# Attention between two expert stages: one reduction on VectorE issued a step earlier, a fourth buffer for the split exponentials, and a small scaling moved to GpSimd

## The chip, the cores and the metric

One core of a Trainium2 chip. The metric is the device time of one execution in microseconds (us), here the median of three. The engines are TensorE (PE in the profile; PEld its weight loads), VectorE (DVE), ScalarE (ACT), GpSimd (POOL) and SyncE (SP), which issues most of the DMAs.

## The reference

Cut to what matters: eight heads of attention over 576 positions for a batch of two, with a bias that comes from a small network over relative positions, and then two pairs of dense layers over the 1152 tokens.

```python
scores = np.matmul(q, k.transpose(0, 1, 3, 2)) / np.sqrt(D)    # B=2, H=8, S=576, D=64
scores = scores + bias.transpose(2, 0, 1)[None]                # bias: a 32-wide net over positions
scores = scores - np.max(scores, axis=-1, keepdims=True)
attn = np.exp(scores)
attn = attn / (np.sum(attn, axis=-1, keepdims=True) + 1e-09)
x = np.matmul(attn, v)                                         # -> [1152, 512]
h = x @ w_in; x = (P(h) / (Q(h) + 1e-6)) @ w_out               # 512 -> 2048 -> 512, rational function
h = x @ w_in2; out = np.maximum(0.01 * h, h) @ w_out2          # 512 -> 2048 -> 512
```

## The kernel before

The program has three stretches. Up to about 60 us it builds the bias tables. From there to about 212 us it runs attention. The rest, two thirds of the time, is the two dense stages, which TensorE fills. Single-precision products are made of three half-precision or rounded products (a high and a low part of each operand).

**Units, tiles and steps.** Attention works on eight units; a unit is a pair of heads in one batch. A unit has nine score tiles: four blocks of 128 rows for each of the two heads (tiles 0 to 7), and a ninth with the last 64 rows of both. The loop goes over all 72 tiles in order, one tile a step, so a unit takes nine steps. Here "step m of a pass" is the step in which the tile number m of the pass's unit is reduced; pass u belongs to unit u.

At each step the program issues, in this order: `qk` of the next tile (six matmuls, line 751, into one of two PSUM slots), `ttr` of this tile (VectorE, line 763: adds the bias, finds the row minimum), `hi` of the tile before (the exponentials rounded to 16 bits into the tile `hl`, ScalarE line 801 or VectorE line 803), `lo` of the tile before that (the remainder of that rounding, line 816, mostly GpSimd, in part VectorE), then the background work due at the step, and `exps` of this tile (ScalarE, line 779). Each engine runs what was issued to it strictly in that order.

**The split exponentials.** Two tiles share one `hl` buffer. When both of its `lo` are done SyncE issues one DMA transpose (line 822) from `hl` into `et`, which the product with v reads later. A `hi` that opens a new `hl` buffer waits until the transpose out of the buffer's former contents has landed. There are `NHL` = 3 such buffers of 4,608 bytes in each partition.

**Background work.** `PLAN` lists it: an entry (step, name) runs for unit i at step 9i + step. The entries that the change and the prediction touch:

- `v_sum` (line 686), now at -4: five matmuls (line 691) that form the squares of v's entries, and a VectorE reduction of the diagonal (line 694), written to `vsc`. It writes and reads a spare corner of `pr`, the PSUM tile of unit i-2. At the same step, and issued ahead of it, stand `rbc` of unit i-2 (twelve short matmuls in the profile, lines 870 and 872) and `prep_q` (ScalarE, line 670).
- `v_scale` (line 698) at -3: one matmul pair (line 701) sums `vsc` over the partitions, ScalarE makes a scale of it (lines 702 and 703). `prep_v8` (line 707) and `prep_vd` (line 711) use the scale at steps 1 and 2 of the unit's own pass.
- `prep_k` at -2 (ScalarE line 682, GpSimd line 683), `prep_ql` at -3 and -1 (VectorE line 675).
- `rmul` (line 885) and `xlo` (line 894), both VectorE, at the step where `rsum` stands.
- `rsum` at 9, that is step 0 of the next pass: a VectorE `tensor_scalar` (line 849) over the nine row sums of the unit, 128 x 9 numbers. `rrec` (line 853), one step later on VectorE, takes the reciprocal, and `rbx` (line 859) one step after that turns it for the rows' normalisation.

For the first two units `v_sum` and `v_scale` stand elsewhere (in the bias stretch), and the last two units take their `rsum` from a second list, `TAIL`. So `PLAN` issues six `v_sum` (units 2 to 7), in passes 1 to 6, and six `rsum` (units 0 to 5), also in passes 1 to 6.

Of the kernel before, what the change touches and what calls it, by code (L numbers as in the profile page):

```python
# [15 lines left out]
ALU = mybir.AluOpType  # L16
# [189 lines left out]
def arrange(tasks, ends, free, shift, slack):  # L206
# [22 lines left out]
    while todo:  # L229
# [36 lines left out]
GROUPS_0 = [[(0, 0), (0, 1)], [(1, 0), (1, 1)], [(2, 0), (2, 1)], [(3, 0), (3, 1)], [(8, 2)]]  # L266
AV_ORDER = (0, 1, 2)
RBX_ACT = True
NHL = 3
LAG_HI, LAG_LO = 1, 2  # L270
PLAN = [(-24, 'load_part', 0), (-22, 'load_part', 1), (-20, 'load_part', 2), (-18, 'load_part', 3), (14, 'rbc'), (17, 'av', 2, 0, 1), (22, 'xhi'), (-2, 'prep_k'), (18, 'rmul'),
        (16, 'av', 1, 0, 1), (1, 'prep_v8'), (-3, 'v_scale'), (17, 'rev'), (11, 'rbx'), (-4, 'v_sum'),
        (12, 'av', 0, 0, 1), (10, 'rrec'), (-1, 'prep_ql', 1), (2, 'prep_vd'), (27, 'xlo'),
        (-4, 'prep_q', 0), (9, 'rsum'), (-2, 'prep_q', 1), (-3, 'prep_ql', 0)]
TAIL = [(2, 'rbx', 0), (3, 'rbc', 0), (2, 'w_load', -2, 0), (1, 'av', 0, 0, 0, 1), (0, 'rsum', 0),
# [73 lines left out]
def attn_bias_moe_kernel(  # L349
# [13 lines left out]
    V, A, G, PE, SP = nc.vector, nc.scalar, nc.gpsimd, nc.tensor, nc.sync  # L363
# [286 lines left out]
    st_q, st_v, kts, ets, vds, vscs = {}, {}, {}, {}, {}, {}  # L650
# [64 lines left out]
    with att, ExitStack() as st:  # L715
# [4 lines left out]
        s_ps, s_pt, s_hl, sums, xx = {}, {}, {}, {}, {}  # L720
# [20 lines left out]
        def kind(i):  # L741
            return (i > 0) + (i == len(units) - 1)
# [49 lines left out]
        def hi(i, j):  # L792
            if group_of[kind(i), j][0] == 0:
                s_hl[i] = hlp.tile([128, most, 2 * S], F16, tag="hl", name="hl", bufs=NHL)
            s_hl[i, j] = s_hl[i]
# [50 lines left out]

        def rsum(i):
            r9 = opn.tile([128, 9], F32, tag="r9", name="r9", bufs=2)
            V.tensor_scalar(r9, sums.pop(i), 1e-9, vscs[i][:, 1:2], ALU.add, ALU.mult)
            r9s[i] = r9  # L850

        def rrec(i):
# [38 lines left out]
        def xlo(i, c=None):  # L891
# [6 lines left out]
        nu = len(units)  # L898
        ops = {
            f.__name__: f  # L900
            for f in (load, load_part, prep_v8, prep_vd, prep_q, prep_ql, prep_k)
            + (av, rsum, rrec, rbx, rbc, rev, rmul, xhi, xlo)
        }

# [131 lines left out]

        hlp = st.enter_context(tc.tile_pool(name="hlp", bufs=NHL))
        etp = [st.enter_context(tc.tile_pool(name=f"etp{x}", bufs=1)) for x in range(2)]
# [363 lines left out]
```

## Time and profile before

| | |
|---|---|
| median of 3 runs | 640.57 us (638.73 to 642.4) |
| the profiled execution | 638.54 us, its span 636.7 us |
| TensorE, VectorE, ScalarE, GpSimd busy over the span | 90%, 86%, 69%, 43% |
| mean granted TensorE clock | 0.973 |

How to read it: the busy shares are means over stretches with different limits, so the part that the change touches is read by itself, in windows of some 17 to 19 us. A row of the timeline is start, duration, engine, line, what it writes and reads, and in brackets how long the engine stood idle before it and what it waited for. A profiled execution is 1.84 us longer than its span.

### The profile page before, as it was taken

What the parts mean: (1) busy time and instruction counts of PE and PEld (TensorE: products, weight loads), DVE (VectorE), ACT (ScalarE), POOL (GpSimd) and SP (SyncE); (2) the same over time, 40 slices, a digit from 0 to 9 for tenths busy, and PEclk for the clock granted to TensorE, in tenths of its full rate; (3) what the DMA queues carried; (4) which work ended last, traced back from release to release, by engine and by line L of the source; (5) the groups of instructions that cost most, each with busy time, mean ns of one, the idle gap of its engine ahead of it and who ended that gap; (6) DMA issues with size and microseconds to landing.
All of it is one profiled execution on the core that took longest, in us unless ns stands there. A gap on an engine that the chain in (4) does not pass through costs nothing.

```text
span 636.7 us, 10678 instructions
## 1 busy us (share of the span) xinstructions
PE 572.0 (90%) x4042; PEld 431.6 (68%) x4042; DVE 545.2 (86%) x818; ACT 438.5 (69%) x705; POOL 270.9 (43%) x194
## 2 busy tenths in 40 slices
PE   4889698888897866799999999999899999999997
PEld 1335577777786756699999999987555555555543
DVE  7997877888887679889999999889897888988684
ACT  8998888888897558898777778648767443444320
POOL 2000866677666124667656766540332112112110
PEclk9999799898999977999999999999999999999999
DMA  6889999999789420132131211031313132131003
GB/s 221 221 219 252 191 174 195 190 190 207 135 162 203 138 99 34 66 113 86 67 133 44 90 67 67 33 133 68 132 71 129 67 117 81 67 132 67 1 0 148
DMA packets 103796, 76.58 MB, mean 120 GB/s; under 512 B 86585, under 2 KB 89145, under 8 KB 103746
## 3 DMA queue, kind: packets, MB, share of 16 engines
q1 hardware_dynamic: 103026, 71.91, 43.7%
q10 hardware_dynamic: 720, 4.00, 1.9%
q8 instruction: 31, 0.51, 0.4%
q14 instruction: 19, 0.16, 0.1%
HBM read 41.69 MB, written 2.36 MB: 69 GB/s over the span
## 4 chain that ended last, share of the span: by engine, by line
PE 50%; DVE 21%; ACT 16%; DMA 6%; issue 5%; SPq 0%; POOL 0%; DVEq 0%; ACTq 0%
PE ph L528 20%; PE pz L1150 14%; PE py L1088 10%; DMA et<-hl 3%; PE ps L751 3%; ACT ex L779 3%; DMA bias<-bb 3%; DVE s L605 2%; DVE pt L763 2%; DVE raw L443 2%; ACT mk L984 2%; DVE raw L441 2%; ACT hl L801 2%; ACT ah L564 1%; DVE mk L986 1%
## 5 line engine op out<-in xcount | busy, mean ns | idle before, releaser
L816 POOL TENSOR_TENSOR hl<-ex,hl 128x512 f16<-128x512 f32 (+2 forms) x94 | 91.0, 986 | 85.4 <-DVE hl L803 54.5
L528 PE MATMUL ph<-bias,bias 128*128 128x384 f32 x576 | 108.6, 346 | 11.6 <-DVE s L602 9.4
L528 PEld LDWEIGHTS ph<-bias,bias 128*128 128x128 f32 x576 | 104.5, 196 | 13.8 <-issue 10.3
L528 PE MATMUL ph<-x,w 128*128 128x384 f16 x576 | 102.0, 326 | 2.1 <-ACT w L489 1.4
L1150 PE MATMUL pz<-w,g 128*128 128x512 f16 (+1 forms) x438 | 101.4, 376 | 1.5 <-DVE bias L1169 1.5
L632 POOL TENSOR_TENSOR g<-s,g 128x1152 f16<-128x1152 f32 x16 | 38.5, 2406 | 144.4 <-ACT g L628 144.4
L751 PE MATMUL ps<-kt,qz 128*128 128x288 f32 x432 | 79.8, 326 | 20.7 <-DVE mn L763 13.9
L751 PEld LDWEIGHTS ps<-kt,qz 128*128 128x128 f32 x432 | 63.6, 200 | 33.8 <-DVE mn L763 18.0
L528 PEld LDWEIGHTS <-w 128*128 128x128 f16 x576 | 55.3, 98 | 45.4 <-issue 4.9
L1088 PE MATMUL py<-gh,wo 128*128 128x384 f32 x288 | 79.9, 340 | 1.7 <-ACT gh L618 1.3
L1150 PEld LDWEIGHTS <-g 128*128 128x128 f16 x438 | 42.7, 98 | 47.2 <-issue 2.0
L779 ACT ACTIVATE ex<-pt,mn 128x576 f32<-128x576 f32 x72 | 55.2, 767 | 9.7 <-DVE mn L763 9.3
L1169 DVE SCALAR_TENSOR_TENSOR bias<-pz,inv,bias 128x512 f32<-128x512 f32 x56 | 41.8, 747 | 22.1 <-PE pz L1150 19.0
L1088 PEld LDWEIGHTS py<-gh,wo 128*128 128x128 f32 x288 | 52.6, 188 | 5.2 <-DVE bias L1100 3.3
L763 DVE CUSTOM_DVE_ANT_0 pt<-ps,bias 128x576 f32<-128x576 f32 x64 | 47.5, 744 | 6.5 <-PE ps L751 2.3
L1088 PE MATMUL py<-gl,wo 128*128 128x384 f32 x156 | 52.2, 335 | 0.0
L599 POOL TENSOR_TENSOR qq<-qq,r 128x1152 f32<-128x1152 f32 (+1 forms) x17 | 41.2, 2429 | 19.0 <-ACT qq L593 14.7
L986 DVE TENSOR_SCALAR mk<-te,off 128x576 f32<-128x576 f32 x108 | 47.1, 507 | 0.0
L439 DVE TENSOR_SCALAR raw<-biasr 128x1024 int32<-128x1024 int32 (+1 forms) x36 | 39.7, 1104 | 6.2 <-DMA biasr<-in_moe_w_in 5.5
L623 POOL TENSOR_TENSOR gl<-s,gh 128x1152 fp32r<-128x1152 f32 (+1 forms) x17 | 41.1, 2427 | 9.0 <-ACT gh L618 8.8
L443 DVE SCALAR_TENSOR_TENSOR raw<-biasr,raw 128x1024 int32<-128x1024 int32 (+1 forms) x36 | 42.2, 1173 | 0.9
L441 DVE SCALAR_TENSOR_TENSOR raw<-biasr,raw 128x1024 int32<-128x1024 int32 (+1 forms) x36 | 40.5, 1126 | 0.7
(131 smaller groups left out, 1095.9 us busy)
## 6 DMA issues: line engine op xcount, KB each, us to landing
biasr<-in_moe_w_in SPq DMA_DIRECT2D x32, 512.0 KB, 4.1
biasr<-in_moe_w_out SPq DMA_DIRECT2D x32, 512.0 KB, 3.2
bias<-bb SPq DMA_DIRECT2D x32, 288.0 KB, 4.7
qkv<-in_qkv ACTq DMA_DIRECT2D x4, 896.0 KB, 7.3
qkv<-in_qkv SPq DMA_DIRECT2D x16, 224.0 KB, 3.1
out<-bias SPq DMA_DIRECT2D x8, 256.0 KB, 2.0
biasr<-bb SPq DMA_DIRECT2D x8, 144.0 KB, 4.6
et<-hl SPq DMA_TRANSPOSE x40, 4.9
```

What stands on the lines that cost most here:

```text
L441: V.scalar_tensor_tensor(bits, hi32, -0x40000000, bits, ALU.bitwise_and, ALU.bitwise_or)
L443: V.scalar_tensor_tensor(bits, lo32, 29, bits, ALU.logical_shift_right, ALU.bitwise_or)
L528: PE.matmul(ps[:, c, 0:CH], w[:, sl], x[kk][:, c * CH:(c + 1) * CH], start=(kk == 0 and n == 0), stop=(kk == KD - 1 and n == 2),)
L599: G.tensor_tensor(part(qq[f], c), part(qq[f], c), part(r0[f], c), ALU.mult)
L751: PE.matmul(ps[:, c, 0:288], lt[:, a], kts[i][:, b, 288 * c:288 * c + 288], start=(n == 0), stop=(n == 2),)
L763: V.tensor_tensor_reduce(out=c2(pt), in0=s_ps.pop((i, j))[:, :, 0:288], in1=c2(bsrc), op0=ALU.add, op1=ALU.min, scale=1.0, scalar=3.0e38, ...
L779: A.activation(et, pt, AF.Exp, bias=mn, scale=-1.0, accum_out=sums[i][:, col:col + 1],)
L816: engines[j in at].tensor_tensor(hl[:, xs, dst], e9[:, xs, src], hl[:, xs, src], ALU.subtract)
L986: V.tensor_scalar(mk, src, off[:, col], 0.0, ALU.add, ALU.max)
L1088: PE.matmul(ps[:, 0:CH], w[:, sl], gts[f][x][:, cs], start=(f == f0 and m == 0), stop=(f == f0 + nf - 1 and m == 2),)
L1150: PE.matmul(ps[:, part], gts[f][x][:, sl], w[:, part], start=(f == f0 and m == 0), stop=(f == f0 + nf - 1 and m == 2),)
L1169: V.scalar_tensor_tensor(dst, ps[:, part], back, dst, ALU.mult, ALU.add)
```

## The change

Three edits, each in one place:

- `NHL` goes from 3 to 4: a fourth `hl` buffer; the tiles that are laid out behind it in the partition move up by 4,608 bytes.
- `v_sum` goes from step -4 to -5. At that step only `xhi` (ScalarE, line 889) of unit i-3 stands ahead of it; `rbc` and `prep_q` of step -4 now come after it. `v_scale` stays at -3.
- `rsum` of units 0 to 5 is issued to GpSimd; units 6 and 7 stay on VectorE. `rrec` stays on VectorE and now has to wait for GpSimd.

```diff
-NHL = 3
+NHL = 4
 PLAN = [...
-        (16, 'av', 1, 0, 1), (1, 'prep_v8'), (-3, 'v_scale'), (17, 'rev'), (11, 'rbx'), (-4, 'v_sum'),
+        (16, 'av', 1, 0, 1), (1, 'prep_v8'), (-3, 'v_scale'), (17, 'rev'), (11, 'rbx'), (-5, 'v_sum'),
...
         def rsum(i):
             r9 = opn.tile([128, 9], F32, tag="r9", name="r9", bufs=2)
-            V.tensor_scalar(r9, sums.pop(i), 1e-9, vscs[i][:, 1:2], ALU.add, ALU.mult)
+            (G if i < nu - 2 else V).tensor_scalar(r9, sums.pop(i), 1e-9, vscs[i][:, 1:2], ALU.add, ALU.mult)
             r9s[i] = r9
```

## Rows read from the trace of the kernel before

**Rows 1.** Busy by pass 3 to 6: window; length, PE PEld DVE ACT POOL; clock; DMA

```profile
111.05:130.03 18.98, 16.56 (x166) 13.88 (x160) 15.90 (x35) 15.87 (x35) 13.04 (x14) 0.91 1.05 189
130.03:147.43 17.40, 15.03 (x161) 12.80 (x159) 15.34 (x35) 15.47 (x34) 13.23 (x14) 1.00 0.98 196
147.43:166.48 19.05, 16.69 (x166) 14.00 (x160) 15.14 (x35) 15.73 (x34) 12.73 (x14) 0.91 0.99 179
166.48:183.94 17.46, 15.08 (x165) 12.87 (x160) 15.30 (x35) 15.66 (x35) 13.21 (x14) 1.00 0.80 151
```

**Rows 2.** Waits from 75 to 200 us: waiter <- releaser, total us, times, longest

```profile
PE ps L751 <- DVE mn L763: 11.7, 14, 2.0
DVE vd L694 <- PE pr L691: 10.7, 6, 1.8
...
ACT vsc L702 <- PE pr L701: 3.1, 3, 1.1
...
ACT hl L801 <- DMA et<-hl: 2.7, 3, 2.1
DVE hl L803 <- DMA et<-hl: 2.0, 3, 1.2
```

**Rows 3.** Timeline of VectorE: `rsum` of pass 2, then of pass 3, and what follows

```profile
94.39 0.23 DVE L849 TENSOR_SCALAR r<-sums,vsc 128x9 f32<-128x9 f32 x1
...
95.21 0.77 DVE L803 CAST hl<-ex 128x576 f16<-128x576 f32 x1
...
96.02 0.69 DVE L763 CUSTOM_DVE_ANT_0 pt<-ps,bias 128x576 f32<-128x576 f32 x1
...
113.22 1.12 DVE L849 TENSOR_SCALAR r<-sums,vsc 128x9 f32<-128x9 f32 x1
114.26 0.74 DVE L763 CUSTOM_DVE_ANT_0 pt<-ps,bias 128x576 f32<-128x576 f32 x1
...
114.94 0.45 DVE L803 CAST hl<-ex 128x576 f16<-128x576 f32 x1
...
115.43 0.69 DVE L763 CUSTOM_DVE_ANT_0 pt<-ps,bias 128x576 f32<-128x576 f32 x1
```

**Rows 4.** Timeline of GpSimd at the same two places

```profile
94.50 4.86 POOL L816 TENSOR_TENSOR hl<-ex,hl 128x512 f16<-128x512 f32 x5 [0.19 <-POOL hl L816]
...
112.67 1.91 POOL L816 TENSOR_TENSOR hl<-ex,hl 128x512 f16<-128x512 f32 x2 [0.20 <-POOL hl L816]
```

**Rows 5.** The chain that ended last, in order of time: one piece, in pass 4

```profile
132.25 1.04 DVE r L849
```

**Rows 6.** Timeline of TensorE after `rsum`: pass 3, then pass 6

```profile
115.06 1.45 PE L751 MATMUL ps<-kt,qz 128*128 128x288 f32 x6 [1.98 <-DVE mn L763]
...
170.50 1.05 PE L751 MATMUL ps<-kt,qz 128*128 128x288 f32 x6 [1.98 <-DVE mn L763]
```

**Rows 7.** Timeline of TensorE in pass 1, steps 5 to 7

```profile
86.66 0.46 PE L691 MATMUL pr<-qkv 128*128 128x128 bf16 x5
86.93 1.04 PE L751 MATMUL ps<-kt,qz 128*128 128x288 f32 x6
87.81 0.28 PE L701 MATMUL pr<-vsc,ones 128*128 128x1 f32 x2
88.28 0.90 PE L751 MATMUL ps<-kt,qz 128*128 128x288 f32 x5 [0.20 <-DVE mn L763]
```

**Rows 8.** Timeline of ScalarE, pass 2: its longest wait for a buffer

```profile
103.67 0.69 ACT L801 ACTIVATE hl<-ex 128x576 f16<-128x576 f32 x1 [2.09 <-DMA et<-hl]
```

**Rows 9.** GpSimd's groups by form over the span: busy us, mean ns | idle before

```profile
L683 POOL TENSOR_TENSOR kt<-qkv,kt 128x576 fp32r<-128x576 f32 x8 | 12.2, 1522 | 12.1 <-ACT kt L682 12.1
L816 POOL TENSOR_TENSOR hl<-ex,hl 128x64 f16<-128x64 f32 x23 | 9.2, 399 | 0.0
...
L962 POOL MEMSET tiny<- 128x1 f32 x1 | 0.1, 108 | 0.0
```

**Rows 10.** GpSimd's first TENSOR_TENSOR of the execution, in the timeline

```profile
8.73 2.06 POOL L683 TENSOR_TENSOR kt<-qkv,kt 128x576 fp32r<-128x576 f32 x1 [5.46 <-ACT kt L682]
```

## The prediction

> **What bounds the kernel now.** The dense stages are TensorE's and hold nothing that the edits touch; they only start earlier or later. So I first cut attention into passes. There [rows 1] no engine is full: in a pass of 17.40 us ScalarE is busy for 15.47, VectorE 15.34, TensorE 15.03, GpSimd 13.23. The pass is a ring of four engines that hand each other tiles, and what counts is which wait ends last at each place. Two things are to be seen. Passes 3 and 5 last 18.98 and 19.05 us, 4 and 6 only 17.40 and 17.46, at nearly the same work: in the long ones the granted TensorE clock is 0.91 on average and TensorE is busy 1.5 to 1.7 us longer. And the list of waits [rows 2] is led by TensorE waiting for the row minimum (11.7 us) and by VectorE waiting for the five matmuls of `v_sum` (10.7 us). The first is a loss. The second looks like one, and the chain has to say whether it is: it holds `rsum`, as a piece of 1.04 us [rows 5], while around `v_sum` it runs through ScalarE or TensorE, not through VectorE.
>
> **rsum.** Nine numbers per partition should be cheap: in pass 2 the instruction takes 0.23 us. In pass 3 it takes 1.12 us [rows 3], and so in four of the six passes that are changed (3 to 6). In pass 2 it started just ahead of GpSimd's `lo`; in pass 3 `lo` had been running since 112.67, 0.55 us before it [rows 4]. So it stood behind GpSimd's instruction. The next tile's reduction came 1.04 us late (113.22 to 114.26), TensorE stood idle for 1.98 us at just this place [rows 6], and ScalarE's next exponential waited too.
>
> Removing it frees 1.04 us of VectorE, but not all stays free. After the next reduction VectorE casts (`hi` of tile 0), and in pass 2, where `rsum` slipped through, that cast took 0.77 us rather than 0.45 [rows 3]: the wait for GpSimd is handed on. From the start of `rsum` to the reduction after the cast it is 2.21 us in pass 3 and 1.63 in pass 2. So one bound of the gain is 2.21 - 1.63 = 0.58 us a pass, the other 1.04. TensorE and ScalarE wait for the earlier reduction, which gains the whole 1.04, VectorE's own line for the later one; I take 0.8, in four passes 3.2 us. In passes 1 and 2 at most the 0.23 goes: together 0.3. Sum 3.5, bounds 2.3 and 4.6.
>
> [...]
>
> On GpSimd the trace shows no tensor_scalar. The nearest rows are a fill of one column, 0.108 us, and a two-operand instruction of 64 columns, 0.399 us [rows 9]. Nine columns are nearer the former; I take 0.2, six times 1.2 us of GpSimd. What hides it: GpSimd is free for 4 us of a pass [rows 1]. Queued behind it are `lo` of tile 8 and its transpose, read much later by the product with v; without that cover it would cost the 1.2 us, 2.4 by the upper row. `rrec` on VectorE now waits for GpSimd. `rsum` can run when `lo` of tile 7 ends, 0.20 us before 112.67 [rows 4]; VectorE comes to `rrec` between the cast (114.94) and the reduction at 115.43 [rows 3], or 1.04 earlier if all the gain arrives. That is over 1 us of slack, so I cost the new wait at nothing; an instruction of more than 1.5 us would use it up.
>
> **TensorE's clock.** In pass 3, behind the 1.98 us of idleness, six matmuls took 1.45 us; in pass 6, behind the same 1.98, they took 1.05 [rows 6]. The drop to the lower of the two levels follows such a wait in two passes of four. In a long pass it costs 16.56 - 15.03 = 1.53 or 16.69 - 15.03 = 1.66 us of TensorE. If the wait shrinks to about 1 us, the drop should become rarer. I take half of the two drops, 1.5 us; bounds 0 and 3.1.
>
> **v_sum.** VectorE's 1.8 us a pass is the largest number here, and I count almost nothing of it. TensorE's order in steps 5 to 7 is `rbc`, `v_sum`, scores of tile 7, `v_scale`, scores of tile 8 [rows 7]. Moved, it is `v_sum`, scores of tile 6, `rbc`, scores of tile 7, `v_scale`: the same matmuls in sum, so the scores of tile 7 end at the same time, and so does `v_scale`, for which ScalarE waits in three passes (3.1 us in all [rows 2]). Those three are passes in which TensorE came late. VectorE reduces tile 6 some 1.5 us earlier, and then waits for the scores of tile 7 instead: what is late next is TensorE. What remains is the 0.20 us that the scores of tile 8 wait for the reduction of tile 6 [rows 7]; six times that is 1.2. Against it, the reduction of v now stands ahead of tile 5's and holds that back a little, covered by ScalarE's queue; uncovered, the 0.27 us of `v_sum` on TensorE (86.66 to 86.93) would be lost six times, 1.6. I take a gain of 0.4, bounds -1.6 and 1.2. No DMA moves with it, and neither SyncE's nor GpSimd's queue is passed.
>
> **The fourth buffer.** Waits for a buffer are 2.7 us on ScalarE and 2.0 on VectorE [rows 2], most of it one wait of 2.09 us in pass 2 [rows 8]. It lies on ScalarE, which is then busy without a gap, and VectorE's wait for `v_sum` at that place, which would have been next, goes too: of that wait I count 1.4. The rest lies where TensorE is late: 0.2. Sum 1.6, bounds 0.4 and 3.5. The tiles that move by 4,608 bytes change which earlier tiles lie under them; no row prices that, and no edge of attention waits for such a tile visibly, so I cost it at nothing.
>
> **Sum.** 3.5 + 1.5 + 0.4 + 1.6 = 7.0 us. The profiled execution took 638.54, so it would be 631.5; the median of the runs lies 2.03 higher: 633.5 us. The bounds together are a gain of 1.1 (2.3 + 0 - 1.6 + 0.4) and 12.4 (4.6 + 3.1 + 1.2 + 3.5). About 0.5% (3.2 us) is what a measurement of this kernel can tell from no change, that is 637.4 to 643.8.
>
> **Rivals.**
>
> The gain is taken up by the ring. ScalarE is busy for 15.5 to 15.9 us of a pass [rows 1]; if its queue, and not the reduction, sets passes 4 and 6, only the small bound of `rsum` (2.3) and of the buffer (0.4) come through, less part of GpSimd's 1.2: 1 to 3 us, 637.5 to 639.5. For it: in passes 4 and 6 ScalarE is the busiest engine. Against it: ScalarE itself waits for the reduction behind `rsum`.
>
> The clock falls more often, and the kernel becomes slower. Shorter waits elsewhere shift where TensorE is idle; the place is the wait after `rsum` or one newly made before the scores of tile 6. The price of a drop is 1.5 to 1.7 us. Without the clock's term the gain is 5.5, so four drops more, one in each of the passes that have none, take it away, and six more, the last of them at the edge to the dense stage, make it slower by 0.5%: 641 to 645. Against it: pass 6 has none at the longest wait [rows 6].
>
> GpSimd's first tensor_scalar costs a start. Its first two-operand instruction took 2.06 us [rows 10] where the mean of that line is 1.52 [rows 9]: 0.5 us once, 634. [...]
>
> All terms come through in full: 12 us, 628 to 629.
>
> **Chances.** The forecast (629.5 to 637.4) 0.54; all in full 0.08; taken up by the ring 0.23, an eighth of it still under 637.4; GpSimd's start 0.05; clock and slower 0.10, of which 0.07 over 643.8. So faster by over 0.5%: 0.65, within: 0.28, slower: 0.07. The likeliest is 633.5. A range of 628.5 to 641 leaves out about 0.05 below and 0.10 above.
>
> **What the profile after would show.** `rsum` on GpSimd at 0.1 to 0.4 us, and no wait of `rrec` for it. TensorE's wait for the row minimum after it near 1 us instead of 1.98, the cast longer. No wait of `v_sum`'s reduction near 1.8 us, but a wait of VectorE for the scores of tile 7 in its place, and passes 4 and 6 at 16.6 to 16.9. Waits for a buffer gone. Passes 3 and 5 near the others if the clock holds. I am wrong if VectorE's 10.7 us come through as time (then about 625), if the new wait stands in front of tile 5 at the same length, or if the dense stage gives the time back.

## The result, and the profile after

The changed kernel takes 632.71 us (median of 6 runs, 630.55 to 635.57), the kernel before 640.04 (6 runs): a ratio of 0.9886, 95% interval 0.9854 to 0.9918, so 7.3 us or 1.1% faster. The forecast was 633.5. The profiled execution took 633.71 us, its span is 631.9. Some executions of a version are over 1.5% longer than its fastest, at a granted clock of 0.952 to 0.963 (the others of the same versions: 0.960 to 0.976): the ratios leave them out, so that a ratio need not be that of the medians, and the one trace taken in such an execution, of the fourth buffer with `v_sum` (647.42 us), is not read.

By pass, passes 3 to 6 (windows from the first reduction of a pass to that of the next; length, then busy TensorE, its weight loads, VectorE, ScalarE, GpSimd; clock, DMA), the changed kernel:

```profile
108.47:126.95 18.48, 15.29 (x160) 12.86 (x161) 15.56 (x34) 15.63 (x34) 13.89 (x15) 1.00 1.08 196
126.95:143.93 16.98, 15.20 (x160) 12.86 (x161) 15.62 (x34) 15.66 (x34) 13.86 (x15) 1.00 1.08 209
143.93:160.91 16.98, 15.21 (x160) 12.86 (x161) 15.64 (x34) 15.66 (x34) 13.88 (x15) 1.00 1.10 199
160.91:177.89 16.98, 15.21 (x160) 12.85 (x161) 15.62 (x34) 15.66 (x34) 13.88 (x15) 1.00 1.06 180
```

Against [rows 1]: the two passes in which the clock had dropped are back at 1.00, and the two clean ones went from 17.40 and 17.46 to 16.98. Pass 3 is still 18.48 long; there ScalarE waited 1.55 us for a buffer.

The waits that answer to [rows 2]:

```profile
ACT ex L779 <- DVE mn L763: 7.2, 8, 1.7
PE ps L751 <- DVE mn L763: 6.3, 9, 1.0
...
DVE qz L675 <- ACT qz L670: 3.3, 5, 1.9
DVE vd L694 <- PE pr L691: 2.5, 6, 1.2
...
ACT hl L801 <- DMA et<-hl: 1.5, 1, 1.5
...
ACT vsc L702 <- PE pr L701: 0.8, 1, 0.8
```

TensorE's wait for the row minimum fell from 11.7 to 6.3 us, the longest from 2.0 to 1.0; VectorE's at `v_sum` from 10.7 to 2.5; the waits for a buffer from 4.7 to 1.5.

The place of `rsum` in pass 3, to set beside [rows 3] and [rows 4]; first VectorE, then GpSimd, in the timeline of the changed kernel:

```profile
109.82 0.75 DVE L894 TENSOR_TENSOR bias<-xx,bias 128x576 fp32r<-128x576 f32 x1
110.49 0.75 DVE L763 CUSTOM_DVE_ANT_0 pt<-ps,bias 128x576 f32<-128x576 f32 x1
...
111.17 1.11 DVE L803 CAST hl<-ex 128x576 f16<-128x576 f32 x1
112.20 0.20 DVE L853 RECIPROCAL r<-r 128x9 f32<-128x9 f32 x1
112.32 0.69 DVE L763 CUSTOM_DVE_ANT_0 pt<-ps,bias 128x576 f32<-128x576 f32 x1
...
112.94 1.30 DVE L711 SCALAR_TENSOR_TENSOR vs<-qkv,vsc,vs 128x640 f16<-128x640 f32 x1
...
109.84 0.88 POOL L849 TENSOR_SCALAR r<-sums,vsc 128x9 f32<-128x9 f32 x1
110.79 5.08 POOL L816 TENSOR_TENSOR hl<-ex,hl 128x512 f16<-128x512 f32 x5
```

The next reduction follows `xlo` at once (110.49). But `rsum` takes 0.88 us on GpSimd, for it started 0.02 us after `xlo` and ran beside it; in pass 2, where it ran beside a reduction instead, it took 0.28. It pushes `lo` of tile 8 back to 110.79, and the cast, which then meets it, takes 1.11 us. From the first reduction to the one behind the cast it is 1.83 us, where [rows 3] had 2.21 from the start of `rsum`. `rrec` waits for nothing.

Attention ends earlier than before, and a part is lost right behind it. The first matmuls of the dense stage, in the timeline of TensorE, the changed kernel:

```profile
198.92 6.52 PE L528 MATMUL ph<-bias,bias 128*128 128x384 f32 x27
```

and the kernel before:

```profile
205.12 4.97 PE L528 MATMUL ph<-bias,bias 128*128 128x384 f32 x27
```

They start 6.2 us earlier and end 4.65 us earlier; the granted clock of the window 196 to 210 us is 0.88. From there to the end the two traces keep their distance, within 0.2 us. The second trace of the changed kernel (run `full` below) loses more at this place:

```profile
198.90 7.69 PE L528 MATMUL ph<-bias,bias 128*128 128x384 f32 x27
```

From the start of attention's last reduction to the end it takes 438.2 us before, and 439.6 and 442.8 us in the two traces of the changed kernel. So what attention gains is given back in part, and differently from execution to execution; two traces don't say how often.

### The profile page after: what moved, and what is told of

Read it like the earlier page. It is cut to its first block, busy times and chain, and to the rows that moved or that the text cites. A ratio compares the mean times of both kernels' runs of the same rounds, so it can differ in the third digit from the quotient of the medians.

```text
span 631.9 us, 10671 instructions
## 1 busy us (share of the span) xinstructions
PE 570.6 (90%) x4042; PEld 430.5 (68%) x4042; DVE 546.6 (86%) x812; ACT 438.0 (69%) x705; POOL 273.9 (43%) x200
## 4 chain that ended last, share of the span: by engine, by line
PE 48%; DVE 23%; ACT 18%; issue 7%; DMA 3%; POOL 0%; SPq 0%; DVEq 0%; ACTq 0%
PE ph L528 19%; PE pz L1150 14%; PE py L1088 10%; ACT ex L779 4%; DVE mk L986 3%; DVE s L605 3%; ACT hl L801 2%; DVE hl L816 2%; DVE raw L443 2%; PE ps L751 2%; DVE pt L763 2%; ACT ah L564 2%; DVE raw L441 2%; ACT s L568 1%; ACT qq L593 1%
## 5 line engine op out<-in xcount | busy, mean ns | idle before, releaser
L751 PE MATMUL ps<-kt,qz 128*128 128x288 f32 x432 | 78.5, 318 | 17.3 <-DVE mn L763 7.9
L751 PEld LDWEIGHTS ps<-kt,qz 128*128 128x128 f32 x432 | 61.3, 193 | 30.4 <-DVE mn L763 14.3
```

The source lines that it names most:

```text
L751: PE.matmul(ps[:, c, 0:288], lt[:, a], kts[i][:, b, 288 * c:288 * c + 288], start=(n == 0), stop=(n == 2),)
```

## The experiments

The prediction's account (theory A): `rsum` holds half of the gain, buffers and clock a fifth each, `v_sum` nothing. The rivals: VectorE's wait for `v_sum` is the gain (theory B), or the edits pay only together (theory C). Seven kernels make, with the one before, all combinations of the three edits. Each is compared with the kernel before on the same chip.

**One edit alone, and the pair without rsum.** The diffs are those of the change, one at a time.

`rsum` alone:

```diff
-            V.tensor_scalar(r9, sums.pop(i), 1e-9, vscs[i][:, 1:2], ALU.add, ALU.mult)
+            (G if i < nu - 2 else V).tensor_scalar(r9, sums.pop(i), 1e-9, vscs[i][:, 1:2], ALU.add, ALU.mult)
```

> Only rsum of units 0 to 5 goes to GpSimd; three buffers, v_sum four steps ahead. Theory A (the prediction's terms): rsum's own term of 3.5 us and part of the clock's 1.5 come through, so 635 to 637 against 640 before. Theory B (VectorE's wait of 1.8 us a pass for v_sum is what was gained): next to nothing from this alone, 639 to 640, and VectorE's wait for v_sum stays at 10 to 11 us. Theory C (the parts only pay together, since each pass hands the wait on): 638 to 640. In all of them rsum on GpSimd takes about 0.9 us where xlo runs beside it, as in the changed kernel, not the 0.2 of the prediction.

Measured 637.33 us, ratio 0.9965 (0.993 to 1.0): a little above theory A's range, and hardly to be told from no gain. `rsum` takes 0.85 to 0.88 us in five of its six passes, and 0.28 in pass 2.

`v_sum` alone:

```diff
-(-4, 'v_sum')
+(-5, 'v_sum')
```

> Only v_sum moves to five steps ahead. Theory A: a gain of 0.4 us with bounds of -1.6 and 1.2, so 639 to 641; VectorE's wait at v_sum falls from 10.7 to some 2.5 us, and about as much waiting shows up for the scores of tile 7 or for ScalarE's prep_q. Theory B: most of the 7.3 us that the whole change gave, 633 to 635. Theory C: 639 to 640.

Measured 638.61 us, ratio 0.9969 (0.9932 to 1.0006). Theory B falls.

The fourth buffer alone:

```diff
-NHL = 3
+NHL = 4
```

> Only the fourth buffer. Theory A: a gain of 0.4 to 1.6 us, 638.5 to 640; the wait of 2.09 us in pass 2 goes, but VectorE's wait for v_sum takes its place in part. Theory B: nothing, 640. Theory C: nothing, 640, since the wait for v_sum ends at the same time as the wait for the buffer.

Measured 635.39 us, ratio 0.9914 (0.988 to 0.9949). This was expected by none of the theories: the edit that I had at 1.6 us gives 5 of the 7. Its waits (75 to 200 us):

```profile
DVE vd L694 <- PE pr L691: 10.7, 6, 1.8
...
ACT hl L801 <- DMA et<-hl: 1.5, 1, 1.5
```

VectorE waits at `v_sum` as long as ever, and the kernel is faster all the same. Its passes 1 to 4 (the columns as above):

```profile
75.77:92.20 16.43, 16.03 (x156) 13.91 (x157) 13.04 (x32) 13.87 (x30) 10.43 (x12) 0.89 0.98 182
92.20:108.30 16.10, 15.18 (x160) 12.88 (x161) 14.08 (x33) 15.41 (x34) 12.65 (x14) 1.00 1.06 187
108.30:127.30 19.00, 16.61 (x160) 14.02 (x161) 15.33 (x35) 15.66 (x34) 13.33 (x14) 0.91 1.11 196
127.30:144.76 17.46, 15.10 (x160) 12.87 (x161) 15.30 (x35) 15.61 (x34) 13.25 (x14) 1.00 1.10 189
```

Passes 1 and 2 of the kernel before:

```profile
75.75:93.04 17.29, 16.89 (x156) 14.46 (x157) 12.96 (x32) 13.88 (x30) 10.29 (x12) 0.84 0.96 178
93.04:111.20 18.16, 15.45 (x160) 12.91 (x161) 14.42 (x33) 15.41 (x34) 13.05 (x14) 1.00 1.07 194
```

So in these two traces the buffer shortens passes 1 and 2, by 2.9 us together, and leaves passes 3 and 4 as long as in [rows 1].

The fourth buffer and `v_sum`, with `rsum` left on VectorE:

> Both other edits, with rsum left on VectorE. Theory A: 2.0 us of buffer and v_sum, 637 to 639. Theory B: nearly all of the gain, 633 to 634. Theory C: clearly less than the whole change, 636 to 639, but more than the sum of the two edits done alone.

Measured 636.15 us, ratio 0.9958 (0.9923 to 0.9994): not better than the buffer alone, and against theory C less than the two edits alone add up to.

**Two edits, and the whole.** The same diffs, two or all three.

> The changed kernel once more, on the chip and in the hour of the next three, as their yardstick: 632 to 634 where the kernel before takes 640 to 640.5.

Measured 633.69 us, ratio 0.9898 (0.9868 to 0.9927). Its passes 3 to 5 are all 16.97 us long, so the wait of 1.55 us in the first profile is not always there; that this execution took 636.61 us lies behind attention, as shown above.

Buffer and `rsum`:

> The fourth buffer and rsum on GpSimd, v_sum left four steps ahead. The buffer alone gave about 5 us and rsum alone about 3. Theory A, corrected (buffer and rsum hold the gain, moving v_sum is worth under 1 us): 632.5 to 634.5, no different from the whole change. Theory B (VectorE's wait for v_sum counts): 635 to 637. Theory C (the parts pay only together): 635 to 637.

Measured 633.5 us, ratio 0.9897 (0.9856 to 0.9939): all of the gain, with `v_sum` where it was. One of its passes without a wait for a buffer and with the clock at 1.00, pass 4:

```profile
125.94:142.90 16.96, 15.23 (x160) 12.89 (x161) 14.93 (x33) 15.61 (x34) 13.64 (x15) 1.00 1.15 191
```

Beside such a pass of the buffer alone (17.46) it shows what `rsum` is worth there, 0.50 us; beside the whole change (16.98) it shows what moving `v_sum` is worth, nothing.

`v_sum` and `rsum`, with three buffers:

> v_sum moved and rsum on GpSimd, with three buffers. Theory A, corrected: the buffers' 4 to 5 us are missing, 636 to 638, and waits for a buffer grow past the 4.7 us of the kernel before, as passes get shorter and the transposes do not. Theory B: 633 to 635. By the prediction's own term for the buffers (1.6 us): 634.5 to 635.5.

Measured 640.07 us, ratio 0.9988 (0.9955 to 1.0021): nothing is left, which is less than any of the forecasts. The waits for a buffer went from 4.7 us to 7.1:

```profile
DVE hl L803 <- DMA et<-hl: 4.3, 5, 1.7
...
ACT hl L801 <- DMA et<-hl: 2.8, 5, 1.3
```

and its passes 3 to 6 (the columns as above) are

```profile
111.47:131.86 20.39, 17.84 (x144) 15.08 (x146) 15.42 (x33) 16.17 (x34) 14.32 (x15) 0.83 0.97 186
131.86:148.82 16.96, 15.54 (x188) 13.30 (x181) 15.04 (x34) 15.47 (x34) 13.36 (x15) 1.00 0.99 183
148.82:167.81 18.99, 16.63 (x160) 13.91 (x161) 14.33 (x34) 15.74 (x34) 13.35 (x15) 0.91 1.05 189
167.81:184.78 16.97, 15.21 (x160) 12.86 (x161) 15.63 (x33) 15.66 (x34) 13.87 (x15) 1.00 0.92 158
```

Passes 4 and 6 are as short as those of the changed kernel. What is lost lies in passes 3 and 5, where the clock is lower. In pass 3 a wait for a buffer stands ahead of the drop: VectorE is held for 1.72 us before a cast, and then the clock falls (window; length, busy times, clock):

```profile
119.63 0.46 DVE L803 CAST hl<-ex 128x576 f16<-128x576 f32 x1 [1.72 <-DMA et<-hl]
...
118.00:121.00 3.00, 2.26 (x28) 1.81 (x23) 1.37 (x4) 2.19 (x5) 1.20 (x3) 1.00 1.27 204
121.00:125.00 4.00, 3.46 (x19) 3.11 (x20) 3.38 (x8) 3.53 (x7) 3.68 (x5) 0.75 0.97 205
125.00:128.00 3.00, 3.00 (x14) 2.98 (x13) 0.77 (x2) 1.25 (x5) 0.89 (x1) 0.50 1.02 206
```

That the wait brings the drop is not shown. In pass 3 of the changed kernel ScalarE is held for 1.55 us by a buffer, TensorE is then less busy than here, and its clock stays at 1.00:

```profile
119.42 0.69 ACT L801 ACTIVATE hl<-ex 128x576 f16<-128x576 f32 x1 [1.55 <-DMA et<-hl]
...
121.00:124.00 3.00, 2.06 (x32) 1.63 (x30) 2.27 (x6) 2.91 (x9) 2.34 (x3) 1.00 0.93 220
124.00:127.00 3.00, 2.04 (x35) 1.60 (x36) 2.94 (x7) 2.94 (x6) 2.00 (x2) 1.00 1.14 200
```

The eight kernels together, as ratios to the kernel before:

| | three buffers | four buffers |
|---|---|---|
| neither | 1 | 0.9914 |
| `v_sum` moved | 0.9969 | 0.9958 |
| `rsum` on GpSimd | 0.9965 | 0.9897 |
| both | 0.9988 | 0.9898 |

Each edit is done in four of these and undone in four. Its mean effect is the mean of the four differences: the buffer (-0.0086 - 0.0011 - 0.0068 - 0.0090) / 4 = -0.0064, 4.1 us; `rsum` (-0.0035 + 0.0019 - 0.0017 - 0.0060) / 4 = -0.0023, 1.5 us; `v_sum` (-0.0031 + 0.0044 + 0.0023 + 0.0001) / 4 = +0.0009, a loss of 0.6 us. A single ratio has an interval of 0.0035 to either side; if the ratios err independently, a mean of four differences is good to about 0.0025 (an estimate). So the buffer's effect is clear, that of `rsum` is about as large as its error, and that of `v_sum` can't be told from nothing. For `rsum` the numbers lean to theory C: without the buffer it is worth nothing on average (0.0035 gained, 0.0019 lost), with it 2.5 us. But the difference between the two is within their error, and passes 4 and 6 above are as short with three buffers.

**Is it the buffer, or where tiles lie?** A new theory: a buffer is occupied from its first `hi` to the landing of its transpose, and three of them are just too few. A rival is that the tiles behind it moved by 4,608 bytes. An unused tile of that size, with three buffers:

```diff
         hlp = st.enter_context(tc.tile_pool(name="hlp", bufs=NHL))
+        pad = st.enter_context(tc.tile_pool(name="pad", bufs=1)).tile([128, most, 2 * S], F16, name="pad")
+        V.memset(pad[:, 0, 0:2], 0.0)
```

> The kernel before with three buffers and an unused tile of 4,608 bytes where the fourth would lie, so that everything behind it lies where it does in the changed kernel (two columns of the unused tile are filled once). Buffer theory: no change, 639.5 to 641. If the gain of the fourth buffer came from where the tiles behind it lie: 635 to 636.

Measured 641.46 us, ratio 1.0001 (0.9956 to 1.0045). Placement is out. And two buffers:

```diff
-NHL = 3
+NHL = 2
```

> The kernel before with two buffers instead of three. Buffer theory: a buffer is taken from its first hi to the landing of its transpose, about 9 us in the trace of before (first hi of a pass at 114.94, its transpose issued at 118.75, landed some 5 us later), and a pass needs five, so with two a pass can't be under 5/2 x 9 = 22 us: 4 to 5 us more in each of eight passes, 670 to 680, and the waits for a buffer ten times as long. If the waits for a buffer were slack that other waits take over, as the prediction had it for all but 2.7 us: 645 to 655.

Measured 681.01 us, ratio 1.0645 (1.0587 to 1.0704), passes 1 to 6 of 21.7 to 24.2 us. The waits for a buffer are now second and third in the list (75 to 230 us):

```profile
ACT hl L801 <- DMA et<-hl: 42.9, 18, 5.0
DVE hl L803 <- DMA et<-hl: 20.8, 8, 3.7
```

The estimate from the time that a buffer is occupied, 5/2 x 9 us, was about right (22 us a pass; the total lies 1 us above the range). With three it gives 5/3 x 9 = 15 us, less than a pass, and yet single waits of up to 2.09 us stand in the trace. A likely reason is that the five buffers of a pass aren't taken at even distances (the ninth tile has one to itself); this is argued, not shown. A fifth buffer was not run, so whether it would still help is open; with four, 0 to 1.5 us of such waits are left on ScalarE and VectorE.

**Is rsum's 0.88 us on GpSimd worth removing?** On ScalarE, units 0 to 5 (the added 1e-9 is left out there):

```diff
+            if i < nu - 2:
+                A.activation(r9, sums.pop(i), AF.Copy, scale=vscs[i][:, 1:2])
+            else:
```

> The changed kernel with rsum of units 0 to 5 on ScalarE instead of GpSimd, as a copy with the scale (the added 1e-9, which is below the last digit of these sums, is left out). If the 0.88 us that rsum takes on GpSimd, and with it the later start of lo of tile 8 and the cast of 1.1 us behind it, are on the path: the cast falls back to 0.5 to 0.8 us, passes 3 to 6 shorten by 0.3 to 0.5 us each, 630.5 to 632. If ScalarE, at 15.6 us of a 17 us pass, is what bounds: 0.25 us more of it in six passes, 633 to 634.5. rsum itself about 0.25 us, as the scale's short instructions on ScalarE.

Measured 633.17 us, ratio 0.9891 (0.9856 to 0.9926). `rsum` takes 0.29 us there, the cast behind it 0.74, and passes 4 to 6 are 16.78, 16.78 and 16.61 us long, 0.2 to 0.4 shorter. So a part of the first forecast holds by the passes, and ScalarE does not bound; but the time as a whole can't be told from that of the change. The same with `v_sum` back at four steps:

> Four buffers and rsum of units 0 to 5 on ScalarE (the added 1e-9 left out), v_sum left four steps ahead: the changed kernel without the edit that showed no gain, and without GpSimd's 0.88 us. Buffer theory: 632.5 to 634, like the whole change; VectorE's wait at v_sum of 1.8 us a pass is back and costs nothing. If moving v_sum pays once the rest is short: 635 to 636.

Measured 635.77 us, ratio 0.9929 (0.9898 to 0.9959). VectorE waits 10.7 us at `v_sum` again, and passes 3 to 5 take 16.62, 16.77 and 17.10 us, no more than with `v_sum` moved (17.66, 16.78, 16.78). By the passes the move is worth nothing here either. The ratio is higher than that of the version before it, but the intervals overlap; and in the two traces the difference lies behind attention, where it takes 442.4 us from the last reduction to the end against 437.9. And on GpSimd, but with `rsum`, `rrec` and `rbx` one step later:

```diff
-(9, 'rsum') ... (10, 'rrec') ... (11, 'rbx')
+(10, 'rsum') ... (11, 'rrec') ... (12, 'rbx')
```

> The changed kernel with rsum, rrec and rbx each one step later, so that GpSimd does lo of tile 8 first. If rsum's 0.88 us ahead of lo of tile 8 delays the cast and with it passes 3 to 6: the cast behind it back at 0.5 to 0.8 us instead of 1.1, 0.3 to 0.5 us a pass, 631 to 632.5. If not: 632.5 to 634.5.

Measured 633.32 us, ratio 0.9902 (0.987 to 0.9934). The timeline in pass 3, first GpSimd, then VectorE:

```profile
112.53 0.28 POOL L849 TENSOR_SCALAR r<-sums,vsc 128x9 f32<-128x9 f32 x1
...
111.52 0.74 DVE L803 CAST hl<-ex 128x576 f16<-128x576 f32 x1
...
112.99 1.75 DVE L711 SCALAR_TENSOR_TENSOR vs<-qkv,vsc,vs 128x640 f16<-128x640 f32 x1
```

`rsum` is 0.28 us and the cast 0.74 instead of 1.11, as expected. But `prep_vd`, next on VectorE with two operands, takes 1.75 us, beside GpSimd's `lo` (112.89 to 116.36), where the changed kernel has 1.30 (at 112.94): what the cast gained is lost behind it, and passes 3 and 4 take 17.10 and 17.09 us, none of the 0.3 to 0.5 us gained (in this trace, whose mean clock is 0.968, pass 5 is 18.89 us long, and in pass 6 the clock falls). None of these versions beats the changed kernel by more than its interval.

## Why the prediction was right, and which steps were not

The time, its sign and its size were right; the shares were not, and two errors cancel.

- **rsum: mis-sized.** The term was 3.5 us (0.8 in each of four passes). By the undisturbed passes it is 17.46 - 16.96 = 0.50 us (buffer alone against buffer and `rsum`), four times 2.0; by the eight kernels it is 2.5 with four buffers and about nothing with three. The step that failed is the weight, "I take 0.8": the lower bound, 0.58 a pass, was the better value, since the cast behind it runs beside GpSimd's `lo` and takes 1.11 us, against 0.45 in [rows 3], where no `lo` ran beside it. That VectorE's instruction stands behind GpSimd's was the author's reading of the longer times; the times are what the traces show. GpSimd's price failed as well, at a smaller cost. I took 0.2 us, between a fill and a two-operand instruction; measured 0.88, outside both rows (0.108 and 0.399), where it ran beside `xlo`, a VectorE instruction with two operands, and 0.28 beside a reduction. I had looked at one direction only: VectorE's `rsum` beside GpSimd's `lo` (1.12 us against 0.23), and not GpSimd's beside a VectorE instruction (0.88 against 0.28). With `rsum` off GpSimd the undisturbed passes were 0.2 to 0.4 us shorter.
- **The fourth buffer: mis-sized.** 1.6 us predicted (0.4 to 3.5), 4.1 measured as a mean, 5 alone. The step that failed is "it lies on ScalarE ... of that wait I count 1.4. The rest lies where TensorE is late": I priced the waits in the list one by one. In the trace of the buffer alone passes 1 and 2 together are 2.9 us shorter; over all traces that are read they take 34.2 to 35.5 us with three buffers (five traces) and 32.5 to 34.2 with four (seven). The rest of the 4.1 lies partly in the clock (next point); it is not laid out wait by wait.
- **The clock: the right place, but not the only one.** Both drops of passes 3 and 5 went; in them TensorE is 1.3 and 1.5 us less busy than before, where I took half of 3.1 us. The order in time bears out the place that the prediction named, the wait behind `rsum`. In the four traces that are read with `rsum` on VectorE (before, `v_sum` alone, buffer alone, unused tile) this wait of 1.98 or 1.99 us stands in each of passes 3 to 6, and all five drops there begin in the first or second six matmuls behind one, so behind 5 of 16. The two levels are 1.00 and 0.50: in the trace before 1249 of 1260 windows of half a microsecond (0 to 630 us) show one of the two, and from 116 to 118 and from 154 to 156 us, in its two drops, it is 0.50. With the buffer alone, in pass 3 (0.91 over the pass):

```profile
112.16 1.07 PE L751 MATMUL ps<-kt,qz 128*128 128x288 f32 x6 [1.98 <-DVE mn L763]
...
113.48 1.81 PE L751 MATMUL ps<-kt,qz 128*128 128x288 f32 x6
```

  What I did not see is that with three buffers a drop comes without that wait. With `rsum` alone on GpSimd it falls later in pass 3 (0.91 from 107.78 to 126.98 us), after VectorE was held for 1.92 us by a buffer:

```profile
120.35 1.06 PE L751 MATMUL ps<-kt,qz 128*128 128x288 f32 x6 [1.25 <-DVE mn L763]
...
123.08 1.62 PE L751 MATMUL ps<-kt,qz 128*128 128x288 f32 x6
```

  With both edits passes 3 to 6 have no drop in any of three traces (the two of the change, and buffer and `rsum`); of the three versions that vary `rsum` further one has a drop, in pass 6. What exactly brings a drop is not settled, and most versions have one trace.
- **v_sum: right, but for where the wait went.** 0.4 us predicted, no gain measured, though VectorE's wait fell by 8 us. The matmuls came in the order that was named. The wait did not come back for the scores of tile 7 (0.6 us in all), as the prediction had it, but behind `prep_q` (3.3 us) and in front of casts.
- **The rivals.** "Taken up by the ring" is what happened with three buffers (0.9988 for the two other edits), but not through ScalarE's queue: with 0.29 us more in it the passes became shorter. "The clock falls more often" has its share at the edge to the dense stage, where one trace gave back 1.55 us and the other more. GpSimd's first tensor_scalar shows no cost of a start: it took 0.67 us, beside a VectorE instruction with two operands, and the later ones 0.28 or 0.88. (At the 634 us that the prediction gave for this rival its chance belonged to "faster", not to "within".)
- **The signs.** Missed besides `rsum`'s own time: passes 4 and 6 at 16.98 us, just above 16.6 to 16.9, and one wait for a buffer of 1.55 us that kept pass 3 at 18.48.

## What to carry to other kernels

A ring of buffers should be sized by the time that one is occupied, from its first write to the landing of the DMA that empties it, and with room to spare: here the mean (15 us for a pass of 17) said that three were enough, and yet a fourth gave 4 to 5 us, more than the waits in the list were priced at. A gain made elsewhere can be lost again while such waits remain. A long wait of one engine is worth nothing if the work behind it is late for another reason too: 8 us of waiting at `v_sum` left the list, and no pass became shorter. An instruction moved to another engine has to be priced beside what runs at that moment on both engines, not by its size: the same 128 x 9 numbers took GpSimd 0.28 us or 0.88.

## What the runs showed of the hardware

A GpSimd tensor_scalar over 128 x 9 numbers took 0.88 us beside a VectorE instruction with two operands in SBUF, and 0.28 us beside a reduction that reads PSUM and SBUF. TensorE's granted clock fell behind 5 of 16 waits of 1.98 or 1.99 us, in the kernel before from 1.00 (112.5 to 115 us) to 0.50 (116 to 118). With `v_sum` and `rsum` moved and three buffers it fell to 0.50 (125 to 128 us) with no single wait of TensorE over 1 us since 109 us, after 2.26 of 3 us busy; in the changed kernel it stayed at 1.00 through 2.06 and 2.04 of 3 us busy.
